# A two-layer recurrent-memory transformer on one core: half 0's last bank in one copy, half 1's scores together, the last 64 dimensions of the ordinary weighting as quarters of the array, up weights loaded sooner

## The chip, the cores and the metric

The kernel runs on one NeuronCore of a Trainium2 chip. The metric is the device time of one execution in microseconds (us), as the median of several runs. The engines are called as the profile calls them: PE is TensorE's matmuls, PEld its weight loads, DVE is VectorE, ACT is ScalarE, POOL is GpSimd and SP is SyncE, which issues most DMAs.

## The reference

There are two layers, each an attention with a recurrent memory and then a gated feed-forward block, over 2048 tokens of 448 numbers.

```
def _A_ref(x, mem0, Wq, Wk, Wv, Wo, seg_len):        # H=16 heads of 256, M=8 memory tokens, segments of 32
    for s in range(n_seg):                            # 64 segments, one after another
        h = concatenate([mem, x[segment s]])          # 40 tokens
        q, k, v = h @ Wq, h @ Wk, h @ Wv
        p = softmax(where(mask, q k^T * scale, -1e9)) # all may look at the 8 memory tokens, causal otherwise
        o = (p @ v) @ Wo
        mem = o[:, :8];  out_s = o[:, 8:]             # the memory goes to the next segment
def _B_ref(x, W_gate, W_up, W_down):                  # 448 -> 1792 -> 448
    g = x @ W_gate;  g = g * (g > 0);  return (g * (x @ W_up)) @ W_down
x = x + A(layernorm(x));  x = x + B(layernorm(x));  x = x + A(layernorm(x));  x = x + B(layernorm(x))
```

The memory makes the segments a chain: segment s+1 needs the output of segment s.

## The kernel before, in words

**Folding.** Before the first segment the weights of each head are multiplied together: Wq Wk^T for the scores (`A_sb`) and Wv Wo for the output (`B_sb`). That is the first stage, about 75 us: loop one over `p` (eight pairs of heads, transposes of Wq and Wk, products `aps`, `mxw`), loop two over `p` (transposes of Wv, products `bps`). `load_wo` fetches a piece of Wo (448 KB) on POOL's queue ahead of loop two, `flips` allocates the transposed tiles `qT`, `kT`, `vT` from a ring of buffers under the tag `tT`.

**Steps.** Then `step(g, ...)` runs for g = 0 to 68. Chain 0 is layer one at segment g, chain 1 is layer two at segment g - 4 (`LAG`), so the steps 4 to 63 carry two chains (80 token columns) and the eight steps 0 to 3 and 64 to 67 carry one (40 columns). Every second step from g = 3 on is a feed step: it carries `ff`, an object `Feed`, whose feed-forward work is placed by hand between the attention's. The other steps are called ordinary here.

**One step on PE**, in order of issue, which `in_order` fixes for PE and `InOrder` for DVE and ACT:
- `project(0, ...)`: the projections of the heads of half 0, five PSUM banks `prj` of up to six head tiles each, called by their first tile 0, 6, 24, 12, 18. Each bank is copied to `TQ` or `TZ` by ACT or DVE. In a feed step the bank 18 of half 0 (`quick`) is copied in two pieces by ACT, the first after three of its six tiles. In a feed step the layernorm's `residual` and `norm` for the feed-forward lie in this stretch (`otp`, then DVE, POOL and DVE again: `xn`).
- `project_early(1, ...)`: a 64-row part of half 1, as pairs of row tiles of the array.
- `late()`: `weigh_x(1)` of the step before, that is the ordinary weighting of half 1: `y1` (two passes of 256 columns for each chain) and `y2` (one of 256, then two of 128 columns for the last 64 dimensions, `hk[rows, 3]` and `hk[rows, 4]`, whose other halves are zero). Chain 0 uses array rows 0 to 63, chain 1 rows 64 to 127, so the two chains' matmuls run side by side.
- `project(1, ...)`, with the memory's scores of half 0 (`scores_m(0)`, bank `Sm`) and their softmax in between.
- `scores_x(0)` (bank `Sx`), the weighting by memory `weigh_m(0)` (`ya`, `yb`), `scores_m(1)`, `scores_x(1)`. Scores run over `KD = (0, 1, 3, 2)`; index 2 needs the last bank's copy.
- In a feed step the gate and up products (`open_rows`, `gate_up`, PSUM tiles `ups`, `gps`, result `hh`) and the down product (`dps`); in both kinds the output projection (`ox`, 84 matmuls for each half, and `o3` in 64-column tiles), with transposes `pps` of the softmax (`flipped`) in between.
- `finish()`, `project_early(0)` of the next step, and `weigh_x(0)`.

**Banks and loads.** `bank(...)` gives out the eight PSUM banks in the program's order, each matmul that opens a bank waits for the copy that last read it. The weights of the feed-forward come in 28 `pieces`, one for each call of `next_piece()`, on SP's queue: 7 of W_up, 7 of W_gate (224 KB each), 14 of W_down (112 KB each). `spread` makes each wait for the PE instruction before it in the program.

Of the kernel before, what the change touches and what calls it, by code (L numbers as in the profile page):

```python
# [8 lines left out]
BF = mybir.dt.bfloat16  # L9
# [8 lines left out]
NP = 8  # L18
# [41 lines left out]
def build_kernel(ctx, tc, A_x, A_mem0, A_Wq, A_Wk, A_Wv, A_Wo, B_W_gate, B_W_up, B_W_down, out,  # L60
# [150 lines left out]
    B_sb = glob.tile([P, 2, NT, DM], BF, name="B_sb")  # L211

    hTb = []
    for i in range(2):
# [58 lines left out]
    with tc.tile_pool(name="pre", bufs=6) as pre:  # L273
# [33 lines left out]
        def flips(src, p, name):  # L307
            nat = load_nat(src, p, nc.sync)
            o = pre.tile([P, 4, 512], BF, tag="tT", name=name)

            def half(e2):
                tp = bank([P, 2, 512], BF, "tpw")
                n = 3 if src is Wv else 4
                for kd in range(n):
                    for e in range(2):
                        tr(tp[:, e, kd * 128:(kd + 1) * 128],
                           nat[:, kd, (2 * e2 + e) * 128:(2 * e2 + e + 1) * 128], ident[:])
                n = DM if src is Wk else 128 * n
# [30 lines left out]
        def load_wo(p):  # L349
            wos.append(pre.tile([P, 4, DM], BF, tag="wo", name="wo", bufs=4))  # L350
            spread(nc.gpsimd.dma_start(wos[-1][:], Wo[:, 4 * p:4 * p + 4, :]))
# [6 lines left out]
        for p in range(NP):  # L358
# [28 lines left out]
            share(A_sb[0:64, 3, hf, 24 + p4, :], mx_ps[0:64, 3, :], 128, (1.28, 0.85))  # L387
            if p >= 4:
                load_wo(p - 4)
            if p == 1:  # L390
# [4 lines left out]
        for p in range(NP):  # L395
            hf, p4 = divmod(p, 4)
            vT = ready
            ready, todo = flips(Wv, p + 1, "vT") if p + 1 < NP else (None, [])
            wo = wos.pop(0)
            for eo in range(2):  # L400
                for kd in range(3):
                    bps = bank([P, 512], F32, "bps")
                    for t in range(2):
                        e = 2 * eo + t
                        mm(bps[:, 0:DM], vT[:, e, kd * 128:(kd + 1) * 128], wo[:, e, :],
                           start=(t == 0), stop=(t == 1))
                    share(B_sb[:, hf, tidx(kd, eo, p4), 0:DM], bps[:, 0:DM], DM, (1.28, 0.85))
                    if kd == 1 and todo:
                        todo.pop(0)()
            bps = bank([P, 512], F32, "bps")  # L410
            for t in range(2):
                for eo in range(2):
                    e = 2 * eo + t
                    mm(bps[64 * eo:64 * eo + 64, 0:DM], v3[:, p, e, :], wo[:, e, :],
                       start=(t == 0), stop=(t == 1), tile_position=(0, 64 * eo))
            share(B_sb[:, hf, 24 + p4, 0:DM], bps[:, 0:DM], DM, (1.28, 0.85))
            if p + 4 < NP:
                load_wo(p + 4)

# [23 lines left out]
    Wg_sb = main.tile([P, 4, F], BF, name="Wg_sb")  # L443
    Wu_sb = main.tile([P, 4, F], BF, name="Wu_sb")
    Wd_sb = main.tile([P, FT, DM], BF, name="Wd_sb")
    pieces = []
    for dst, src in ((Wu_sb, B_W_up), (Wg_sb, B_W_gate)):
        for k in range(3):
            for cols in (slice(0, F // 2), slice(F // 2, F)):
                pieces.append((dst[:, k, cols], src[128 * k:128 * k + 128, cols]))  # L450
        pieces.append((dst[FR[src is B_W_gate], 3, :], src[384:448]))
    for f in range(FT):
        pieces.append((Wd_sb[:, f, :], B_W_down[128 * f:128 * f + 128]))

    def next_piece():

        if pieces:
            spread(nc.sync.dma_start(*pieces.pop(0)))


# [133 lines left out]
    def project(hf, chains, hb, j, banks, pre={}, busy=False, first=None, inside=None):  # L594

        n = L * len(chains)
        for i0, k in banks:
            ps = pre[i0] if i0 in pre else bank([P, 512], F32, "prj")
            two = len(chains) == 2
            quick = busy and not hf and i0 == 18  # L600

            def copies(eng, rows, T, a, b):
                T = T.rearrange("p g (t q) -> p t g q", q=16)
                if two:
                    evac(eng, T, ps[rows, a * n:b * n].rearrange("p (t g q) -> p t g q", t=b - a, q=16))
                    return
                c = chains[0]
                src = ps[rows, a * n:b * n].rearrange("p (t w) -> p t w", t=b - a)
# [5 lines left out]
            def tq(a, b):  # L614
                return TQ[hf][:].rearrange("p g u w -> p g (u w)")[:, :, 16 * (i0 + a):16 * (i0 + b)]

            for i in range(k):
                if inside is not None and i == 4:
                    inside()
                if quick and i == 3:  # L620
                    copies(act, slice(0, P), tq(0, 3), 0, 3)
                for kd in range(3 if i0 in pre else 4):
# [7 lines left out]
            if i0 < 24:  # L630
                a = 3 if quick else 0
                copies(act if (i0 != 6 if busy and hf else i0 % 12) else dve, slice(0, P), tq(a, k), a, k)
            else:
                copies(act if busy else dve, slice(0, 64), TZ[hf][0:64, :, 0:64], 0, k)
                copies(act, slice(64, 128), TZ[hf][64:128, :, 64:128], 0, k)
            if i0 in (6, 18):
# [43 lines left out]
    def step(g, ff, pre, late):  # L680
# [28 lines left out]

        def scores_m(hf):  # L710
            if not ms:
                return (lambda: None,) * 3
            Sp = bank([P, 2, L], F32, "Sm", 1100)
            for kd in KD:
                mm(Sp[:, :, :], queries(hf, 2, kd), moving(hb, j, kd, (0, 1)), start=(kd == KD[0]), stop=(kd == KD[-1]))
            return softmax(Sp, 2, PM[hf], blk[:], f"m{hf}")

        def scores_x(hf):
            Sp = bank([P, 4, L], F32, "Sx", 2500 if hf == 0 else 3500 if ff is None else 8000)
            both = len(chains) == 2  # L720
            if not both:
                mm(Sp[:, :, :], ident[:], maskS[:], start=True, stop=False, skip_group_check=True)
            for half in range(2):
                for c in chains:
                    for kd in KD:
                        mm(Sp[:, 2 * half + c, :], queries(hf, 3 * c + half, kd), moving(hb, j, kd, (c,)),
                           start=(both and kd == KD[0]), stop=(kd == KD[-1]), skip_group_check=True)
            return softmax(Sp, 4, PX[hf], None, f"x{hf}", maskS[:] if len(chains) == 2 else None)

# [12 lines left out]

        def weigh_x(hf, hk, PT):

# [13 lines left out]
            for c in chains:  # L758
                keep(act if c == 0 or len(chains) == 1 else dve, c, 0, y1[c][:])
            y2 = {c: bank([P, 384], F32, f"y2_{c}", 1300) for c in chains}  # L760
            for c in chains:
                rows = slice(64 * c, 64 * c + L)
                mm(y2[c][:, 0:256], hk[rows, 2, :], PT[rows, 0:256], start=True, stop=True)
            for eo in range(2):
                for c in chains:
                    rows = slice(64 * c, 64 * c + L)
                    mm(y2[c][:, 256:384], hk[rows, 3 + eo, :],
                       PT[rows, :].rearrange("p (e o w) -> p e o w", e=2, o=2)[:, :, eo, :],
                       start=(eo == 0), stop=(eo == 1))
            for c in chains:  # L770
# [76 lines left out]
        pre1 = project_early(1, chains, hb, j)  # L847
        if late is not None:
            late()
        if len(chains) == 1:  # L850
            m0 = scores_m(0)
            m0[0]()
            m0[1]()
        project(1, chains, hb, j, BANKS[1][0:1], pre1, True)
        if len(chains) == 2:
            m0 = scores_m(0)
            m0[0]()
            m0[1]()
        project(1, chains, hb, j, BANKS[1][1:2], pre1, True, m0[2])
# [11 lines left out]
        if ff is not None:  # L871
            ff.xposed_out()
        x0 = scores_x(0)
        weigh_m(0, hk, pm)
        m1 = scores_m(1)
        m1[0]()
        m1[1]()
        x1 = scores_x(1)
        x0[0]()
# [44 lines left out]
        else:  # L924
# [24 lines left out]
        weigh_x(0, hk, px0)  # L949
        return pre, lambda: weigh_x(1, hk, px1)  # L950

# [91 lines left out]
```

## Time and profile before

| | |
|---|---|
| median of 3 runs | 1606.29 us (1604.5 to 1607.28) |
| profiled execution, its own time | 1606.33 us |
| span of its profile | 1604.4 us |
| PE busy, share of the span | 1573.1 us, 98% |
| PE weight loads | 1445.3 us, 90% |
| DVE, ACT, POOL busy | 1133.0, 757.4, 77.4 us |
| TensorE clock granted | full throughout |
| PE, longest class of waits | 16.6 us, 33 times, projections behind ACT's copy to TQ |

The profile's span is 1.93 us shorter than its execution's time. In a timeline row the columns are start (us from the span's start), length (us), engine, line, operation, tiles, array rows * columns used, shape, count, and in brackets the idle time before it and what ended it. A row of xN stands for N instructions in a row; matmuls overlap, a single one of 80 columns is shown as 0.20 us long, but the next starts far earlier. The idle time in brackets is counted from the shown end of the matmul before, so the start of a row says more than the bracket. All matmuls have one line, that of the helper `mm` (L143), transposes another (L151), and copies that of `InOrder` (L101), so rows are told apart by tiles.

### The profile page before, as it was taken

Reading aid. Unit: us, or ns where it says so; the run is one execution under the profiler, and the core shown is the slowest. Engines: PE = TensorE matmul, PEld = TensorE weight load, DVE = VectorE, ACT = ScalarE, POOL = GpSimd, SP = SyncE. Lnnn points to the kernel's source line nnn. Section 1 sums busy time; section 2 is a strip of 40 time slices with the busy share of each in tenths; the row PEclk is TensorE's granted clock in tenths of the full one; section 3 lists DMA queues with packets and bytes.
Section 4 is the critical chain, followed back from the end, with each engine's and each line's share of the span. In section 5 each row is a group of like instructions: output and inputs, shape, how many; then the busy total and the mean of one; then the engine's idle time right before and its main releaser. Section 6 shows DMA issues by size and latency. Waiting matters only on the chain.

```text
span 1604.4 us, 89783 instructions
## 1 busy us (share of the span) xinstructions
PE 1573.1 (98%) x41132; PEld 1445.3 (90%) x41132; DVE 1133.0 (71%) x3706; ACT 757.4 (47%) x2126; POOL 77.4 (5%) x172
## 2 busy tenths in 40 slices
PE   9999999999999999999999999999999999999998
PEld 6688999999999999999999999999999999999897
DVE  8766777777677777776777777767777777667765
ACT  5644444454444444544444445444444454444443
POOL 3200000000000000000000000000000000000000
PEclk9999999999999999999999999999999999999999
DMA  8530000000000000000000000000000000000000
GB/s 242 163 107 15 8 9 9 10 4 9 9 10 9 9 9 9 4 9 10 9 9 9 9 8 5 10 9 9 9 9 9 7 5 10 9 8 6 7 7 6
DMA packets 27755, 33.12 MB, mean 21 GB/s; under 512 B 3560, under 2 KB 26480, under 8 KB 27376
## 3 DMA queue, kind: packets, MB, share of 16 engines
q1 hardware_dynamic: 26288, 23.70, 5.3%
q8 instruction: 321, 5.26, 1.3%
q0 software_dynamic: 1088, 3.68, 0.8%
q14 instruction: 58, 0.48, 0.1%
HBM read 23.70 MB, written 1.84 MB: 16 GB/s over the span
## 4 chain that ended last, share of the span: by engine, by line
PE 96%; ACT 1%; DVE 1%; issue 1%; DMA 0%; SPq 0%; POOLq 0%; ACTq 0%; POOL 0%
PE prj L143 31%; PE ox L143 25%; PE ups L143 7%; PE dps L143 5%; PE gps L143 5%; PE o L143 5%; PE y L143 4%; PE Sx L143 3%; PE pps L151 2%; PE Sm L143 2%; PE bps L143 1%; PE aps L143 1%; PE tpw L151 1%; PE ya L143 1%; PE tps L151 1%; PE yb L143 1%
## 5 line engine op out<-in xcount | busy, mean ns | idle before, releaser
L143 PE MATMUL prj<-hT,A_sb 128*128 128x80 bf16 (+3 forms) x15232 | 547.1, 199 | 17.3 <-ACT TQ L101 16.6
L143 PEld LDWEIGHTS <-A_sb 128*128 128x128 bf16 (+1 forms) x15232 | 500.8, 99 | 42.9 <-issue 21.2
L143 PEld LDWEIGHTS <-B_sb 128*128 128x128 bf16 (+1 forms) x15232 | 490.6, 103 | 14.5 <-issue 1.0
L143 PE MATMUL ox<-Y,B_sb 128*128 128x80 bf16 (+3 forms) x11424 | 440.3, 199 | 0.9 <-issue 0.9
L101 ACT CAST TQ<-prj 128x480 bf16<-128x480 f32 (+5 forms) x416 | 189.6, 466 | 111.4 <-PE prj L143 101.4
L101 DVE CAST Y<-y 128x256 bf16<-128x256 f32 x376 | 151.4, 457 | 55.5 <-PE y L143 55.4
L101 ACT CAST Y<-y 128x512 bf16<-128x512 f32 (+2 forms) x392 | 136.6, 419 | 103.4 <-PE y L143 103.2
L101 ACT ACTIVATE se<-se 128x80 f32<-128x80 f32 (+1 forms) x270 | 81.9, 303 | 165.5 <-DVE se L101 161.2
L143 PE MATMUL gps<-xT,Wg_sb 128*128 128x128 bf16 (+3 forms) x1904 | 133.9, 216 | 0.0
L101 DVE CAST TQ<-prj 128x480 bf16<-128x480 f32 (+1 forms) x228 | 128.4, 572 | 7.5 <-PE prj L143 7.0
L143 PE MATMUL ups<-xT,Wu_sb 128*128 128x128 bf16 (+3 forms) x1904 | 132.3, 216 | 0.5 <-DVE xT L101 0.5
L101 DVE SCALAR_TENSOR_TENSOR hh<-gps,ut 128x512 bf16<-128x512 f32 (+2 forms) x136 | 80.2, 592 | 47.6 <-PE ya L143 41.4
L143 PEld LDWEIGHTS <-Wu_sb 128*128 128x128 bf16 (+1 forms) x1904 | 105.0, 97 | 8.0
L143 PEld LDWEIGHTS <-hk 40*128 40x128 bf16 (+1 forms) x1950 | 99.4, 96 | 10.7 <-issue 2.5
L143 PEld LDWEIGHTS <-Wg_sb 128*128 128x128 bf16 (+1 forms) x1904 | 106.9, 97 | 0.5 <-issue 0.5
L101 ACT CAST TZ<-prj 64x320 bf16<-64x320 f32 (+2 forms) x264 | 96.8, 377 | 17.2 <-DVE TZ L101 13.6
L101 ACT COPY os<-o 64x16 f32<-64x16 f32 (+3 forms) x135 | 25.8, 191 | 162.2 <-PE o L143 160.6
L101 DVE TENSOR_REDUCE ssum<-se 128x2 f32<-128x80 f32 (+1 forms) x270 | 73.7, 273 | 37.5 <-ACT se L101 37.5
L143 PE MATMUL dps<-Wd_sb,hh 128*128 128x448 bf16 (+1 forms) x476 | 93.1, 353 | 0.0
L143 PEld LDWEIGHTS <-TQ 128*128 128x128 bf16 x1938 | 87.1, 97 | 6.0 <-issue 0.4
L143 PE MATMUL y<-PT,hk 40*128 40x256 bf16 (+1 forms) x1280 | 86.7, 248 | 1.6 <-ACT PT L101 1.0
L235 POOL TENSOR_SCALAR rstd<-mv 128x1 f32<-128x1 f32 x67 | 14.8, 221 | 1467.2 <-DVE mv L101 1467.2
(118 smaller groups left out, 1920.0 us busy)
## 6 DMA issues: line engine op xcount, KB each, us to landing
wo<-in_A_Wo_dram POOLq DMA_DIRECT2D x8, 448.0 KB, 4.6
nat<-in_A_Wq_dram SPq DMA_DIRECT2D x8, 384.0 KB, 4.9
nat<-in_A_Wk_dram SPq DMA_DIRECT2D x8, 384.0 KB, 5.0
nat<-in_A_Wv_dram SPq DMA_DIRECT2D x8, 384.0 KB, 5.7
xa<-in_A_x_dram SPq DMA_DIRECT2D x32, 56.0 KB, 2.2
xa<-xp SPq DMA_DIRECT2D x32, 56.0 KB, 1.9
out_dram<-xa SPq DMA_DIRECT2D x32, 56.0 KB, 2.3
xp<-in_A_x_dram SPq DMA_DIRECT2D x30, 56.0 KB, 2.6
```

Of the source, the lines that this page charges most:

```text
L101: r = f(*a, **k)
L143: in_order(nc.tensor.matmul(out, lhsT, rhs, **k))
L151: in_order(nc.tensor.transpose(out, src, idn))
L235: nc.gpsimd.tensor_scalar(out=rstd[:], in0=mv[:, 1:2], scalar1=EPS, scalar2=None, op0=ALU.add)
```

## The change

Five edits, all of the order or the shape of work; what is computed stays.

- `project`: `quick` is gone; bank 18 of half 0 is copied whole in feed steps too, after its sixth tile.
- `scores` takes the place of `scores_m` and `scores_x`. For half 1 it issues memory and ordinary scores together: indices 0, 1, 3 of `Sm`, then of all groups of `Sx`, then index 2 of `Sm`, then of `Sx`.
- `weigh_x`: the last 64 dimensions use 64x64 quarters of the array: stationary `hk[rows, 3, 0:64]`, the even and the odd heads in column halves 0 and 64, so four matmuls of 128 columns stand in four quarters.
- In one-chain steps the memory's scores of half 0 (`memory_0`) stand inside `weigh_x(1)`, between `y1` and `y2`, and `late_flip` is 23 in place of 22.
- `Wu_sb` moves to the pool of the whole kernel, its seven pieces are issued in loop two of the folding (two for each `p` from 3 on), and the pieces of W_gate and W_down take the earlier calls. For the room, `tT` has 4 buffers in place of 6, `wo` has 3 in place of 4, and Wo's pieces are asked for one pair of heads later. In the built program SP's queue still has all loads of Wv ahead of the first piece of W_up.

```diff
+    Wu_sb = glob.tile([P, 4, F], BF, name="Wu_sb")
...
+    pieces = weights(Wu_sb, B_W_up)
...
-            o = pre.tile([P, 4, 512], BF, tag="tT", name=name)
+            o = pre.tile([P, 4, 512], BF, tag="tT", name=name, bufs=4)
...
-            wos.append(pre.tile([P, 4, DM], BF, tag="wo", name="wo", bufs=4))
+            wos.append(pre.tile([P, 4, DM], BF, tag="wo", name="wo", bufs=3))
...
-            if p >= 4:
-                load_wo(p - 4)
+            if p >= 5:
+                load_wo(p - 5)
...
-            if p + 4 < NP:
-                load_wo(p + 4)
+            if p + 3 < NP:
+                load_wo(p + 3)
+            if p >= 3:
+                next_piece()
+                next_piece()
...
+    pieces += weights(Wg_sb, B_W_gate)
...
-            quick = busy and not hf and i0 == 18
...
-                if quick and i == 3:
-                    copies(act, slice(0, P), tq(0, 3), 0, 3)
...
+            if m and x:
+                mem(KD[:3])
+                mask()
+                own(KD[:3])
+                mem(KD[3:])
+                own(KD[3:])
...
             for eo in range(2):
                 for c in chains:
                     rows = slice(64 * c, 64 * c + L)
-                    mm(y2[c][:, 256:384], hk[rows, 3 + eo, :],
+                    mm(y2[c][64 * eo:64 * eo + 64, 256:384], hk[rows, 3, 0:64],
                        PT[rows, :].rearrange("p (e o w) -> p e o w", e=2, o=2)[:, :, eo, :],
-                       start=(eo == 0), stop=(eo == 1))
+                       start=True, stop=True, tile_position=(64 * c, 64 * eo), skip_group_check=True)
...
         if late is not None:
-            late()
-        if len(chains) == 1:
-            m0 = scores_m(0)
-            m0[0]()
-            m0[1]()
+            late(memory_0 if len(chains) == 1 else None)
+        if len(chains) == 1 and late is None:
+            memory_0()
...
-        x0 = scores_x(0)
+        _, x0 = scores(0, False, True)
         weigh_m(0, hk, pm)
-        m1 = scores_m(1)
+        m1, x1 = scores(1, True, True)
         m1[0]()
         m1[1]()
-        x1 = scores_x(1)
...
-            late_flip = 23 if hi - lo == W else 22
+            late_flip = 23
```

More of the change, by code (lines that the diff above doesn't have):

```diff
@@ L211, in build_kernel, with weights, next_piece @@
     B_sb = glob.tile([P, 2, NT, DM], BF, name="B_sb")
+    Wu_sb = glob.tile([P, 4, F], BF, name="Wu_sb")
+    def weights(dst, src):
+        return [(dst[:, k, cols], src[128 * k:128 * k + 128, cols])
+                for k in range(3) for cols in (slice(0, F // 2), slice(F // 2, F))] + [
+                    (dst[FR[src is B_W_gate], 3, :], src[384:448])]
+    pieces = weights(Wu_sb, B_W_up)
+    def next_piece():
+        if pieces:
+            spread(nc.sync.dma_start(*pieces.pop(0)))
     hTb = []
@@ L443, in build_kernel @@
     Wg_sb = main.tile([P, 4, F], BF, name="Wg_sb")
-    Wu_sb = main.tile([P, 4, F], BF, name="Wu_sb")
+    pieces += weights(Wg_sb, B_W_gate)
     Wd_sb = main.tile([P, FT, DM], BF, name="Wd_sb")
[L446 to L451, printed above, removed]
     for f in range(FT):
         pieces.append((Wd_sb[:, f, :], B_W_down[128 * f:128 * f + 128]))
-    def next_piece():
-        if pieces:
-            spread(nc.sync.dma_start(*pieces.pop(0)))
     class Feed:
@@ L599, in project, with copies @@
             two = len(chains) == 2
-            quick = busy and not hf and i0 == 18
-            def copies(eng, rows, T, a, b):
+            def copies(eng, rows, T):
                 T = T.rearrange("p g (t q) -> p t g q", q=16)
                 if two:
-                    evac(eng, T, ps[rows, a * n:b * n].rearrange("p (t g q) -> p t g q", t=b - a, q=16))
+                    evac(eng, T, ps[rows, 0:k * n].rearrange("p (t g q) -> p t g q", t=k, q=16))
                     return
                 c = chains[0]
-                src = ps[rows, a * n:b * n].rearrange("p (t w) -> p t w", t=b - a)
+                src = ps[rows, 0:k * n].rearrange("p (t w) -> p t w", t=k)
                 x, m = (0, SEG) if c == 0 else (MEM, 0)
@@ L612, in copies @@
                      src[:, :, x:x + SEG].rearrange("p t (g q) -> p t g q", q=16))
-            def tq(a, b):
-                return TQ[hf][:].rearrange("p g u w -> p g (u w)")[:, :, 16 * (i0 + a):16 * (i0 + b)]
             for i in range(k):
@@ L630, in project @@
             if i0 < 24:
-                a = 3 if quick else 0
-                copies(act if (i0 != 6 if busy and hf else i0 % 12) else dve, slice(0, P), tq(a, k), a, k)
-            else:
-                copies(act if busy else dve, slice(0, 64), TZ[hf][0:64, :, 0:64], 0, k)
-                copies(act, slice(64, 128), TZ[hf][64:128, :, 64:128], 0, k)
+                T = TQ[hf][:].rearrange("p g u w -> p g (u w)")[:, :, 16 * i0:16 * (i0 + k)]
+                copies(act if (i0 != 6 if busy and hf else i0 % 12) else dve, slice(0, P), T)
+            else:
+                copies(act if busy else dve, slice(0, 64), TZ[hf][0:64, :, 0:64])
+                copies(act, slice(64, 128), TZ[hf][64:128, :, 64:128])
             if i0 in (6, 18):
@@ L708, in hk_make, with scores, mem, own @@
             return hk
-        def scores_m(hf):
+        def scores(hf, m, x):
             if not ms:
[L712 to L719, printed above, removed]
-            both = len(chains) == 2
[L721 to L728, printed above, removed]
+                m = False
+            both = len(chains) == 2
+            Sm = bank([P, 2, L], F32, "Sm", 1100) if m else None
+            Sx = bank([P, 4, L], F32, "Sx", 2500 if hf == 0 else 3500 if ff is None else 8000) if x else None
+            groups = [(half, c) for half in range(2) for c in chains]
+            def mem(kds):
+                for kd in kds:
+                    mm(Sm[:, :, :], queries(hf, 2, kd), moving(hb, j, kd, (0, 1)),
+                       start=(kd == KD[0]), stop=(kd == KD[-1]), skip_group_check=True)
+            def own(kds):
+                for half, c in groups:
+                    for kd in kds:
+                        mm(Sx[:, 2 * half + c, :], queries(hf, 3 * c + half, kd), moving(hb, j, kd, (c,)),
+                           start=(both and kd == KD[0] and (half, c) == groups[0]), stop=(kd == KD[-1]),
+                           skip_group_check=True)
+            def mask():
+                if not both:
+                    mm(Sx[:, :, :], ident[:], maskS[:], start=True, stop=False, skip_group_check=True)
+            if m and x:
[4 more added lines that the diff above has]
+                own(KD[3:])
+            elif m:
+                mem(KD)
+            elif x:
+                mask()
+                own(KD)
+            sm = softmax(Sm, 2, PM[hf], blk[:], f"m{hf}") if m else (lambda: None,) * 3
+            sx = softmax(Sx, 4, PX[hf], None, f"x{hf}", maskS[:] if both else None) if x else None
+            return sm, sx
@@ L741, in weigh_m, with weigh_x @@
             act.copy(YB[hf][:, 16:28, M0:M0 + 16], yb[:].rearrange("p (t q) -> p t q", q=16))
-        def weigh_x(hf, hk, PT):
+        def weigh_x(hf, hk, PT, between=None):
             def keep(eng, c, t0, src):
@@ L759, in weigh_x @@
                 keep(act if c == 0 or len(chains) == 1 else dve, c, 0, y1[c][:])
+            if between is not None:
+                between()
             y2 = {c: bank([P, 384], F32, f"y2_{c}", 1300) for c in chains}
@@ L847, in step, with memory_0 @@
         pre1 = project_early(1, chains, hb, j)
-        if late is not None:
-            late()
-        if len(chains) == 1:
-            m0 = scores_m(0)
+        m0 = None
+        def memory_0():
+            nonlocal m0
+            m0, _ = scores(0, True, False)
             m0[0]()
             m0[1]()
+        if late is not None:
+            late(memory_0 if len(chains) == 1 else None)
+        if len(chains) == 1 and late is None:
+            memory_0()
         project(1, chains, hb, j, BANKS[1][0:1], pre1, True)
         if len(chains) == 2:
-            m0 = scores_m(0)
-            m0[0]()
-            m0[1]()
+            memory_0()
         project(1, chains, hb, j, BANKS[1][1:2], pre1, True, m0[2])
@@ L949, in step @@
         weigh_x(0, hk, px0)
-        return pre, lambda: weigh_x(1, hk, px1)
+        return pre, lambda between: weigh_x(1, hk, px1, between)
     nsteps = nseg + LAG
```

## The prediction

> **What bounds the kernel now.** First the page, for the span, the busy times and the chain of work that ended last.
>
> ```profile
> span 1604.4 us, 89783 instructions
> PE 1573.1 (98%) x41132; PEld 1445.3 (90%) x41132; DVE 1133.0 (71%) x3706; ACT 757.4 (47%) x2126; POOL 77.4 (5%) x172
> PE 96%; ACT 1%; DVE 1%; issue 1%; DMA 0%; SPq 0%; POOLq 0%; ACTq 0%; POOL 0%
> ```
>
> PE is the end. Time is won only where PE waits or where it has fewer passes. So next the waits, for PE alone:
>
> ```profile
> PE prj L143 <- ACT TQ L101: 16.6, 33, 0.5
> ```
>
> This is the only class that comes back in every feed step (33 of them); no other class on PE is over 1.2 us. Then the timeline of one feed step around it:
>
> ```profile
> 710.81 1.21 PE L143 MATMUL prj<-hT,A_sb 128*128 128x80 bf16 x29
> 712.11 0.36 ACT L101 CAST TQ<-prj 128x240 bf16<-128x240 f32 x1
> 712.52 1.02 PE L143 MATMUL prj<-hT,A_sb 128*128 128x80 bf16 x33 [0.50 <-ACT TQ L101]
> 712.78 0.61 DVE L101 TENSOR_SCALAR xn<-xa,mv,rstd 128x448 bf16<-128x448 bf16 x2 [0.39 <-POOL rstd L236]
> 713.04 0.36 ACT L101 CAST TQ<-prj 128x240 bf16<-128x240 f32 x1 [0.57 <-PE prj L143]
> 713.37 0.61 PE L143 MATMUL y<-PT,hk 40*128 40x256 bf16 x10
> 713.82 1.22 DVE L101 CAST Y<-y 128x512 bf16<-128x512 f32 x3 [0.44 <-PE y L143]
> 713.91 0.82 PE L143 MATMUL prj<-hT,A_sb 128*128 128x80 bf16 x18
> ```
>
> PE stops after three of the six tiles of bank 18 until ACT has read them (712.47), since its next matmul writes the same bank. And the same place in an ordinary step, where the bank is already copied whole:
>
> ```profile
> 739.40 1.13 PE L143 MATMUL prj<-hT,A_sb 128*128 128x80 bf16 x36
> 740.03 0.56 ACT L101 CAST TQ<-prj 128x480 bf16<-128x480 f32 x1 [0.35 <-PE prj L143]
> 740.37 0.65 PE L143 MATMUL y<-PT,hk 40*128 40x256 bf16 x10
> 740.95 0.42 PE L143 MATMUL prj<-hT,A_sb 128*128 128x80 bf16 x7
> ```
>
> **1. `quick` goes.** A matmul of 80 columns is shown 0.20 us long, but x29 take 1.21, so they start (1.21-0.20)/28 = 0.036 us apart. The last before the stop starts at 710.81+1.01 = 711.82, the next at 712.52: 0.70, of which 0.04 is work. The bracket's 0.50 counts from the shown end; PE loses 0.67. Over 33 feed steps: -22.1 us.
>
> What is late next? Two things in the same step. (a) The second bank of `y2` is the bank just copied. The whole copy starts 0.23 after the last matmul of the bank, as in the ordinary step, and takes 0.56 against 0.36. The ordinary step shows the price: from the first `y` to the next `prj` 740.95-740.37 = 0.58, in the feed step 713.91-713.37 = 0.54. So +0.04 to +0.05. (b) DVE is in `xn` until 713.39, set by the layernorm's chain through POOL, which does not move. Its copy of `y1`, now ready for at 713.82-0.67 = 713.15, starts 0.25 late and ends at 714.09. The first matmul into that bank (bank 24 of half 1) starts in the trace at 714.70, after the change at 714.70-0.67+0.05+0.04 (edit 2) = 714.12, and a wait needs some 0.05 from the end of the copy. So +0.02. Together +0.07 on 33 steps, +2.3.
>
> **2. Quarters.** Each call of `weigh_x` loses one pass of 128 columns, 0.055 us (the four `tps` transposes of 128 columns start 0.056 apart), and gains one change of the array's tile shape, from 64x128 to 64x64, ahead of the change back to 128x128 that it has already. The trace has no 64x64 tile, so I take the price from the nearest changes:
>
> ```profile
> 707.12 0.49 PE L143 MATMUL ox<-Y,B_sb 128*128 128x80 bf16 x9
> 707.54 0.60 PE L143 MATMUL prj<-hT,A_sb 64*128 64x80 bf16 x24
> 703.06 1.19 PE L143 MATMUL o<-Y,B_sb 128*64 128x80 bf16 x56
> 704.18 0.60 PE L143 MATMUL ox<-Y,B_sb 128*128 128x80 bf16 x12
> ```
>
> Nine matmuls 0.036 apart from 707.12 would end their turn at 707.44; the row tiles start at 707.54: 0.10. The `o` pairs are again 0.036 apart, the last pair starts at 703.06+1.19-0.20 = 704.05, and `ox` follows at 704.18 and not 704.09: 0.09 to 0.10 for column tiles. The step from 128*64 back to 64*128 tiles (`bps` to `prj`, 75.69) also pays. So rows and columns cost alike, and I take 0.095: net +0.04 per call. There are 2x60 calls with two chains and 16 with one, 136: +5.4 us. Ends: no price for this change -0.055, that is -7.5; a price plus two passes in turn because four quarters do not all run side by side +0.10, that is +13.6. The weight loads speak for side by side: the two column tiles of `o` load in turns and still start as pairs 3 ns apart.
>
> The Trainium skill, "TensorEngine Tiling (Array Packing)", section Key Properties, speaks against this edit: changing the tiling mode, not just the tile, drains the engine. By that rule the quarters lose, and the 0.10 at each change in the rows above agrees; by the same page's "Theoretical Speedup" table alone the edit would be a gain, which is the -7.5 end.
>
> **3. Scores of half 1 together.** The last index of `Sm` waits for bank 18's copy:
>
> ```profile
> 718.19 0.20 PE L143 MATMUL Sm<-hT,TZ 128*128 128x80 bf16 x1
> 718.36 0.21 PE L143 MATMUL Sm<-hT,TQ 128*128 128x80 bf16 x1
> ```
>
> 0.17 against 0.036, so 0.14 in a feed step; in the ordinary step 745.01 to 745.13, so 0.08. After the change twelve matmuls of 0.025, 0.30 us, stand in between and cover it. But `Sm` is then finished some 0.2 later, and DVE's softmax with it. In a feed step DVE runs without a gap from there to `hh` (721.61 to 722.29), and the `gps` that reuses its bank starts at 722.53: DVE comes 0.33 later against PE, the slack is 0.24 less 0.05, so 0.13 of the 0.14 is given back. In the ordinary step `PM1` is ready at 747.66, its transpose at 748.05; it eats the slack and costs 0.01 to 0.02. So -0.01 on 30 feed steps and -0.06 on 30 ordinary ones: -2.1 us.
>
> **4. One-chain steps.** The memory's scores between `y1` and `y2` take away a wait of `Sm` on ACT's copy of `Y` (once, 0.4 by the waits); the later `Sm` of half 1 and the later flip shift a transpose that waits on `PM1` by under 0.1 in five steps. Taken as 0, within 0.5 either way.
>
> **5. Loads.** In the one-chain steps PE's own instruction queue runs dry at times while weights stream in:
>
> ```profile
> 89.94 0.34 PE L143 MATMUL ox<-Y,B_sb 128*128 128x40 bf16 x7 [0.86 <-issue]
> 105.77 0.27 PE L151 MATMUL pps<-ident,PX 128*128 128x128 bf16 x2 [0.56 <-issue]
> ```
>
> There are five such gaps between 85 and 106 us; start to start they lose 3.4 us. They stand beside pieces of W_up and W_gate (224 KB); the step from 106 to 121 us, with pieces of W_down (112 KB) alone, has none. After the change W_gate takes W_up's calls and W_down those of W_gate, so half as much flows from 86 on. I take -1.5, from 0 to -3.4. The cover of the moved pieces is loop two of the folding, where DMA is at 0.24 of its share and PE is in `bps` passes of 0.189 us. SP's queue puts them behind all loads of Wv, so nothing on it waits for them but the next pieces. On POOL's queue Wo is asked for two passes of loop two ahead (2x3.55 us) and lands in 4.0 to 4.3 there; the first, asked for at 39.9, landed at 47.3 and is needed at 48. If it came late it would cost up to 1 us. POOL's clearing of `hk`, `Y1` and `hh` moves from 63.3 to some 67 and takes 5.1, needed from 77 on: 0. The smaller `tT` ring still holds this pass's and the next pass's two tiles: 0.
>
> **Sum.** -22.1+2.3+5.4-2.1+0-1.5 = -18.0. The profiled execution took 1606.33, span 1604.4 and 1.9 around it, and the median is 1606.29, so no correction: 1588.3 us, 1.1% faster. What a measurement can tell from no change is about 0.2%, 3.2 us.
>
> **Rivals.**
> - *The quarters switch for free.* For: both shapes have 64 rows, only the columns change. Against: the 128x64 column tiles pay too. Then 136x0.095 = 12.9 less: 1575.4. Chance 0.10.
> - *The wait moves.* DVE (71% busy) becomes the bound in the feed step: `y1`'s copy behind `xn`, then the softmax. If every later wait kept DVE's lag of 0.42 of the 0.67, 33x0.42 = 13.9 comes back: 1602. Against: the slack of 0.41 at the transpose of `PM0` (717.19, ready 716.77). Chance 0.10.
> - *Slower: four quarter loads in a row.* A tile shape's first weight load can't be hidden behind the shape before it; if the four loads (`LDWEIGHTS` of 128x64 from `B_sb`: 113 ns mean) followed one another, each call would pay 0.095 and three more of 0.10 before its one pass: +0.34, 136 times +46, and 1588.3+46-5.4 = 1629. It decides from (18.0+5.4)/136 = 0.17 per call on. Against: the `o` pairs. Chance 0.05. The same section of the Trainium skill says under Restrictions that column tiling disables fast weight load; no run here shows a 64x64 load.
>
> **Numbers.** Forecast 0.73, rivals 0.10, 0.10, 0.05, unknown 0.02. The forecast's own range is 1582 to 1595 by the ends of edits 2, 4 and 5. With the free switch nearly and half of the moved wait it is 1577 to 1598. Faster 0.92, same 0.03, slower 0.05.
>
> **What would show it.** The class PE prj behind ACT TQ is gone from PE's waits; a feed step is 0.53 shorter, an ordinary one within 0.05 of before. From the first `y` to the next `prj` both kinds take 0.58 to 0.63; 0.49 would be the free switch, 0.9 the loads in a row. No wait over 0.05 ahead of the last `Sm`; a new one of about 0.13 at the second `gps`. Fewer gaps by issue between 85 and 106. Wrong, if PE waits anew for DVE's `Y` or `PM`, or for Wo around 48 us.

## The result

The changed kernel takes 1595.29 us (median of 4 runs, 1593.72 to 1596.08). The kernel before, run beside it, takes 1606.47. The ratio is 0.9931, with an interval from 0.9914 to 0.9948: 11 us faster, where 18 were forecast. The profiled execution took 1594.63 us, its span is 1592.6, so the two profiles differ by 11.8 us.

The page after, its busy times and the chain that ended last:

```profile
span 1592.6 us, 89753 instructions
...
PE 1578.0 (99%) x41132; PEld 1435.4 (90%) x41132; DVE 1133.2 (71%) x3706; ACT 753.6 (47%) x2090; POOL 77.4 (5%) x172
...
PE 97%; DVE 1%; issue 0%; ACT 0%; SPq 0%; DMA 0%; POOLq 0%; POOL 0%; ACTq 0%
```

PE is still the end. Its busy time rose by 4.9 us while the span fell, a first sign that something made its work longer. ACT has 36 instructions fewer: the second pieces of bank 18's copy. The waits of PE, the longest classes:

```profile
PE junk L143 <- DVE still L170: 1.2, 1, 1.2
PE y L143 <- ACT PT L101: 1.0, 2, 0.5
PE pps L151 <- DVE PM L101: 1.0, 2, 0.5
```

The class of 16.6 us, projections behind ACT's `TQ`, is gone, and nothing of its size has come. What came instead is small and hides in starts, not in this view. The timeline of the feed step that the prediction showed:

```profile
705.89 2.56 PE L143 MATMUL prj<-hT,A_sb 128*128 128x80 bf16 x76
...
707.31 0.66 DVE L101 CAST TQ<-prj 128x480 bf16<-128x480 f32 x1
...
708.01 0.56 ACT L101 CAST TQ<-prj 128x480 bf16<-128x480 f32 x1 [0.45 <-PE prj L143]
...
708.29 0.78 PE L143 MATMUL y<-PT,hk 40*128 40x256 bf16 x10
...
708.81 0.11 PEld L143 LDWEIGHTS <-hk 40*64 40x64 bf16 x4 [0.31 <-issue]
...
709.00 0.82 PE L143 MATMUL prj<-hT,A_sb 128*128 128x80 bf16 x18
```

PE now runs through bank 18 without a stop. From the first `y` to the next `prj` it takes 709.00-708.29 = 0.71, where 0.54 was measured before and 0.58 to 0.63 forecast. ACT's whole copy ends at 708.57, and the second bank of `y2` has to wait for it. The same stretch in the other call, `weigh_x(0)` at the end of the same step, where the second bank waits some 0.03 in both kernels:

```profile
730.93 0.72 PE L143 MATMUL y<-PT,hk 40*128 40x256 bf16 x10
731.58 1.47 PE L143 MATMUL prj<-hT,A_sb 128*128 128x80 bf16 x36
```

0.65 us against 0.59 before. The new wait at the second `gps`, in DVE's timeline and in PE's:

```profile
716.86 1.28 DVE L101 SCALAR_TENSOR_TENSOR hh<-gps,ut 128x512 bf16<-128x512 f32 x2
```
```profile
717.42 0.22 PE L143 MATMUL ups<-xT,Wu_sb 64*128 64x128 bf16 x1
717.42 0.22 PE L143 MATMUL gps<-xT,Wg_sb 64*128 64x128 bf16 x1
717.47 0.22 PE L143 MATMUL ups<-xT,Wu_sb 64*128 64x128 bf16 x1
717.60 0.21 PE L143 MATMUL gps<-xT,Wg_sb 64*128 64x128 bf16 x1
```

`ups` and `gps` are row tiles that run side by side, here at 717.42 both. The pair after it is torn apart, 717.47 and 717.60: `gps` waits for the first of the two `hh` (716.86 plus half of 1.28). The bracket shows nothing, since the matmul before is drawn longer than the gap; only the starts do.

Measured from the first `kps` of a step (the transposes near its start) to that of the next, with two chains, a feed step fell from 27.88 to 27.42 us on most steps (-0.445 in the mean) and an ordinary step rose from 18.03 to 18.09 (+0.064).

### The profile page after: what moved, and what is told of

Its sections match the earlier page's. It is cut to its first block, busy times and chain, and to the rows that moved or that the text cites. A ratio compares the mean times of both kernels' runs of the same rounds, so it can differ in the third digit from the quotient of the medians.

```text
span 1592.6 us, 89753 instructions
## 1 busy us (share of the span) xinstructions
PE 1578.0 (99%) x41132; PEld 1435.4 (90%) x41132; DVE 1133.2 (71%) x3706; ACT 753.6 (47%) x2090; POOL 77.4 (5%) x172
## 4 chain that ended last, share of the span: by engine, by line
PE 97%; DVE 1%; issue 0%; ACT 0%; SPq 0%; DMA 0%; POOLq 0%; POOL 0%; ACTq 0%
PE prj L143 31%; PE ox L143 25%; PE ups L143 7%; PE dps L143 5%; PE gps L143 5%; PE y L143 5%; PE o L143 5%; PE Sx L143 3%; PE pps L151 2%; PE bps L143 1%; PE aps L143 1%; PE Sm L143 1%; PE tpw L151 1%; PE ya L143 1%; PE yb L143 1%; PE kps L151 1%
## 5 line engine op out<-in xcount | busy, mean ns | idle before, releaser
L143 PE MATMUL prj<-hT,A_sb 128*128 128x80 bf16 (+3 forms) x15232 | 541.6, 199 | 0.5 <-issue 0.5
L101 ACT CAST TQ<-prj 128x480 bf16<-128x480 f32 (+1 forms) x380 | 184.2, 497 | 113.3 <-PE prj L143 103.0
L143 PE MATMUL gps<-xT,Wg_sb 128*128 128x128 bf16 (+3 forms) x1904 | 137.2, 215 | 0.0
L143 PEld LDWEIGHTS <-hk 40*128 40x128 bf16 (+2 forms) x1950 | 92.5, 98 | 35.8 <-issue 22.8
L143 PE MATMUL y<-PT,hk 40*128 40x256 bf16 (+1 forms) x1280 | 100.4, 258 | 1.9 <-ACT PT L101 1.0
L101 ACT COPY PT<-pps 128x256 bf16<-128x256 bf16 (+1 forms) x136 | 47.2, 347 | 81.8 <-PE pps L151 77.6
```

The costliest lines, as they stand in the source:

```text
L101: r = f(*a, **k)
L143: in_order(nc.tensor.matmul(out, lhsT, rhs, **k))
```

## The experiments

**Each edit alone in the kernel before.** Four runs take the parts of the forecast one by one.

```diff
-            quick = busy and not hf and i0 == 18
+            quick = False
```

> The kernel before, with only bank 18 of half 0 copied whole in feed steps. Theory A (read from the trace after: the shortfall against the forecast is mostly the quarters, and each feed step keeps 0.67 less 0.10 that the second bank of y2 now waits for the copy): 33 x -0.56 = -18.6 us, ratio 0.9884; from the first y to the next prj 0.64 in a feed step against 0.54 before. Theory B (the shortfall lies here, DVE's lag gives much of the 0.67 back later in the step): -12 to -14 us, ratio 0.992, with new waits of PE on DVE (Y, PM or hh) in feed steps. As predicted: -19.8.

Measured: 1590.70 us against 1608.28, ratio 0.9889 (0.9875 to 0.9902), 17.8 us faster. Theory A holds. A feed step is 0.555 shorter, an ordinary one 0.003. So `quick` was worth nearly all of its 0.67 and DVE is no new bound. What is given back is 0.10, not 0.07, in one place, `y2`'s second bank. The timeline of the kernel with this edit alone:

```profile
705.09 0.56 ACT L101 CAST TQ<-prj 128x480 bf16<-128x480 f32 x1 [0.45 <-PE prj L143]
...
705.37 0.71 PE L143 MATMUL y<-PT,hk 40*128 40x256 bf16 x10
...
706.01 0.82 PE L143 MATMUL prj<-hT,A_sb 128*128 128x80 bf16 x18
```

0.64 from `y` to `prj`, where it was 0.54. The copy runs from 705.09 to 705.65; within the x10 row, `y2`'s second bank starts at 705.70, 0.107 behind its partner instead of 0.003. In the ordinary step of before the copy starts 0.34 ahead of the first `y`, here 0.28.

```diff
-                    mm(y2[c][:, 256:384], hk[rows, 3 + eo, :],
+                    mm(y2[c][64 * eo:64 * eo + 64, 256:384], hk[rows, 3, 0:64],
...
-                       start=(eo == 0), stop=(eo == 1))
+                       start=True, stop=True, tile_position=(64 * c, 64 * eo), skip_group_check=True)
```

> The kernel before, with only the last 64 dimensions of the ordinary weighting as 64x64 quarters. Theory A: 136 calls at +0.066 (one more change of tile shape 0.09, the change back from 64x64 some 0.02 dearer, one pass of 0.055 less) = +9.0 us, ratio 1.0056. Theory B: the quarters are nearly neutral, the added time being covered by waits that were there anyway: 0 to +2 us, ratio 1.000 to 1.001. As predicted: +5.4 us, ratio 1.0034. Without a price for the change of shape: -7.5 us, 0.9953.

Measured: 1618.12 us, ratio 1.0058 (1.0045 to 1.0070), 9.3 us slower. Theory A holds. Both kinds of step are 0.134 longer, 0.067 for each call. The call at the end of an ordinary step:

```profile
712.97 0.72 PE L143 MATMUL y<-PT,hk 40*128 40x256 bf16 x10
713.62 1.47 PE L143 MATMUL prj<-hT,A_sb 128*128 128x80 bf16 x36
```

It is 0.65 from `y` to `prj`, as in the changed kernel. A step has two such calls, so 0.134; in the changed kernel the scores give part of it back in an ordinary step, and +0.064 is left.

```diff
-        x0 = scores_x(0)
+        _, x0 = scores(0, False, True)
...
-        m1 = scores_m(1)
+        m1, x1 = scores(1, True, True)
```

> The kernel before, with only half 1's two kinds of scores issued together. Theory A: feed step -0.14 at the last Sm and +0.12 back at the second gps, ordinary step -0.08 and +0.02 back at the first ox: 30 x -0.02 and 30 x -0.066, -2.6 us, ratio 0.9984. Theory B: the later softmax of half 1 also costs at later transposes: 0. If the cover were free in both kinds of step: -6.6 us.

Measured: 1604.93 us, ratio 0.9983 (0.9974 to 0.9992), 2.7 us faster. Theory A holds: feed -0.035, ordinary -0.078. The wait ahead of the last `Sm` (0.14) is gone, and `gps` waits 0.11 for `hh`, where 0.12 was expected.

```diff
+    pieces = weights(Wu_sb, B_W_up)
...
+            if p >= 3:
+                next_piece()
+                next_piece()
...
+    pieces += weights(Wg_sb, B_W_gate)
...
-    pieces = []
```

(in short: the loads, pools and ring sizes of the change, and nothing else of it)

> The kernel before, with only the up weights loaded in the folding, and the smaller rings. Prediction: gaps by issue on PE between 77 and 122 us fall from 3.4 to about 1.9, -1.5 us, ratio 0.9991. Rival: the gaps come from how the instruction queue refills in one-chain steps, whatever is loaded: they move and do not shrink, 0 us.

Measured: 1607.14 us, ratio 0.9992 (0.9983 to 1.0001). The time alone cannot be told from no change. The gaps by issue between 76 and 123 us say more. In the changed kernel:

```profile
PE ox L143 <- issue: 0.9, 1, 0.9
PE prj L143 <- issue: 0.5, 1, 0.5
```

and with the loads alone:

```profile
PE prj L143 <- issue: 0.3, 1, 0.3
PE Sx L143 <- issue: 0.2, 1, 0.2
```

Five profiles with the loads as before add up to 2.3 to 3.7 us of such gaps in this window (mean 2.7), eight with the early loads to 0.3 to 1.9 (mean 1.1). So the early loads are worth 1.6 us, less sharply than forecast: one gap of 0.9 stands at 89.95 as it did before, with half as much weight in flight.

Where the gaps stand says what they are. Between 76 and 123 us the thirteen profiles have 50 of them of more than 0.15 us. Counted in PE's instructions (matmuls and weight loads together) all 50 lie at whole multiples of 256 from one another, to within two, and each ends 1.2 to 1.8 us after the end of a packet of the DMA queue q8. The page of before has this line for that queue:

```profile
q8 instruction: 321, 5.26, 1.3%
```

These are 321 packets of 16 KB, one for every 256 of PE's 82264 instructions. So PE lacked its own next instructions there, as the forecast had it. That the pieces of weights are what holds these packets up is argued from the totals alone.

**The change without its quarters.** The two lines of the second experiment put back in the changed kernel.

> The changed kernel with the last 64 dimensions back in 64x128 row tiles; all else of the change kept. Theory A (each call pays 0.066 for the quarters): 9.0 us less than the changed kernel, ratio to before 0.9875. Theory B (the shortfall is DVE's lag, which the quarters' time only covers, so PE would wait for it instead): within 3 us of the changed kernel, ratio 0.991 to 0.993.

Measured: 1587.00 us against 1607.68, ratio 0.9870 (0.9857 to 0.9884). Theory A holds. This beats both kernels; its interval lies below that of the change. Feed steps -0.579, ordinary -0.073 against before: close to the sum of the first and third experiments (-0.590 and -0.081).

**What the quarters cost: the changes of shape.** The quarters are issued ahead of `y2`'s pass of 256 columns, so that the array goes through 64x128, 64x64, 64x128 and 128x128 tiles.

```diff
-            for c in chains:
-                rows = slice(64 * c, 64 * c + L)
-                mm(y2[c][:, 0:256], hk[rows, 2, :], PT[rows, 0:256], start=True, stop=True)
             for eo in range(2):
...
+            for c in chains:
+                rows = slice(64 * c, 64 * c + L)
+                mm(y2[c][:, 0:256], hk[rows, 2, :], PT[rows, 0:256], start=True, stop=True, skip_group_check=True)
```

> The changed kernel with the quarters ahead of y2's pass of 256 columns, so that the array goes 64x128, 64x64, 64x128, 128x128: one more change of shape, the same matmuls. Theory A (every change between shapes costs about 0.09 to 0.12, both ways): from the first quarter to the pass of 256 columns 0.16 to 0.18 us in place of 0.06; in the late calls this lies beside the 0.10 that y2's second bank waits, in the calls at the step's end it does not, so +3 us to +6 us on the changed kernel, ratio to before 0.995 to 0.997. Rival (the 0.09 is the quarters' own first loads, and the way back between two shapes of 64 rows is free): 0.06 between them, no loss, up to -3 us, ratio 0.991 to 0.993.

Measured: 1602.33 us, ratio 0.9964 (0.9951 to 0.9976). Theory A holds: one more change, 0.077 more in a feed step and 0.121 in an ordinary one than in the changed kernel. These are two calls each, and with two chains a part of the change falls into the wait for `y2`'s second bank; a call with one chain, which has no such wait, takes 0.104 more (0.694 in place of 0.590). `y1`'s last pass to the first quarter takes 0.196, of which 0.105 is the pass: 0.09 for the change between two shapes that both have 64 rows. From the last quarter to the next pass it takes 0.173; if the quarter counts as 0.055, that leaves 0.12.

**What the quarters cost: the passes.** All four quarters are issued twice (the first round's line is that of the added loop, L788).

> The changed kernel with the four quarter matmuls issued twice. Theory A (the four run side by side, the price is in the changes of shape): one more pass of 0.055 to 0.06 for each of 136 calls, +7.5 to +8 us, ratio to before 0.998. Rival (the quarters follow one another, or two by two): +0.11 to +0.22 per call, +15 to +30 us, ratio 1.002 to 1.012.

Measured: 1603.24 us, ratio 0.9974 (0.9964 to 0.9984); 0.11 more for each step than the changed kernel, 0.055 for each call, one pass and not four. The timeline of a call at a step's end (half 0):

```profile
707.03 0.11 PEld L788 LDWEIGHTS <-hk 40*64 40x64 bf16 x4
707.03 0.25 PE L788 MATMUL y<-PT,hk 40*64 40x128 bf16 x4
707.06 0.12 PEld L143 LDWEIGHTS <-hk 40*64 40x64 bf16 x4
707.11 0.23 PE L143 MATMUL y<-PT,hk 40*64 40x128 bf16 x4
707.27 1.46 PE L143 MATMUL prj<-hT,A_sb 128*128 128x80 bf16 x36
```

Four matmuls of 128 columns take one turn, and the second four's loads lie beside the first four's matmuls. The rival of loads in a row falls here. But the second round starts 0.08 after the first (707.03 to 707.11), not 0.055, and from the last quarter to `prj` it now takes 0.148, where the changed kernel takes 0.173.

**An attempt to hide the wait of `y2`'s bank.** In the version without quarters, `project_early` goes between `y1` and `y2` (in the call of `late()`, and in the weighting at the step's end).

```diff
-            late(memory_0 if len(chains) == 1 else None)
+            late(memory_0 if len(chains) == 1 else early_1)
...
+            weigh_x(0, hk, px0, early_0)
```

> A version that should beat both: the changed kernel without the quarters, and in two-chain steps project_early, which is in 64-row tiles too, stands between y1 and y2 of weigh_x, so that y2's second bank is free when PE comes to it. The waits in the late calls (0.10 in feed steps, 0.05 in ordinary ones) and the 0.03 of the calls at the step's end should go: 30 x 0.15 + 60 x 0.03 = 6 us less than the version without quarters, ratio to before 0.984. Rival: the wait moves on to the next bank or to DVE: no gain on the version without quarters, 0.9875.

Measured: 1607.97 us, ratio 1.0003 (0.9994 to 1.0011), 21 us slower than the version without quarters, where 6 us faster were expected. In the call of `late()`, `y2` comes no later than before, since `y1` and the early projections only change places. At the step's end the banks are given out anew, and `y2`'s second bank is that of `y1`. The timeline there:

```profile
735.81 0.59 PE L143 MATMUL prj<-hT,A_sb 64*128 64x80 bf16 x24
736.01 0.59 ACT L101 CAST Y<-y 128x512 bf16<-128x512 f32 x1 [1.34 <-PE y L143]
...
736.24 0.78 PE L143 MATMUL y<-PT,hk 40*128 40x256 bf16 x6
```

Six matmuls that need 0.4 take 0.78: all but the first wait for ACT's copy of `y1`, until 736.60. The wait is 0.40 to 0.46 each time, 60 times, 26 us.

**The wait for `hh`.** In the version without quarters, the ordinary weighting's softmax steps stand ahead of `Sm`'s in feed steps, so that DVE has work while the later `Sm` comes.

```diff
+        if swap:
+            x0[0]()
+            x0[1]()
         m1[0]()
         m1[1]()
-        x0[0]()
+        if not swap:
+            x0[0]()
...
-            x0[1]()
+            x0[2]()
             m1[2]()
-            x0[2]()
```

> The change without its quarters, and in the feed steps the ordinary weighting's maximum, negation and exponentials stand on DVE and ACT ahead of those of the other chain's product Sm, instead of DVE waiting for Sm first. Theory A (the wait of 0.116 us that TensorE takes up at the second chain's scores of a feed step, for the weighting hh, comes from the place of hh behind the late Sm): 30 x 0.116 = 3.5 us off the version without quarters, about 0.985 of the kernel before. Theory B (Sm's own chain, now behind, holds TensorE up just as long at its weighted sum): no gain, 0.987. Slower than 0.988 would mean that Sm's exponentials were needed sooner.

Measured: 1585.07 us, ratio 0.9856 (0.9843 to 0.9870). In the timeline of the version without quarters the pair is torn apart as in the changed kernel:

```profile
714.03 0.22 PE L143 MATMUL ups<-xT,Wu_sb 64*128 64x128 bf16 x1
714.15 0.21 PE L143 MATMUL gps<-xT,Wg_sb 64*128 64x128 bf16 x1
```

and with the new order it is closed to 0.01:

```profile
714.17 0.22 PE L143 MATMUL ups<-xT,Wu_sb 64*128 64x128 bf16 x1
714.18 0.21 PE L143 MATMUL gps<-xT,Wg_sb 64*128 64x128 bf16 x1
```

Nearly every two-chain feed step from g = 7 on is 0.10 shorter than without the edit, so theory A holds there, about 3 us. But the sum is 2 us at most, since `PM` comes late in the first steps. The class in PE's waits, with the new order:

```profile
PE pps L151 <- DVE PM L101: 2.5, 3, 1.1
```

**The one-chain edit alone**, in the kernel before.

```diff
-            late()
-        if len(chains) == 1:
-            m0 = scores_m(0)
+            late(memory_0 if len(chains) == 1 else None)
...
-            late_flip = 23 if hi - lo == W else 22
+            late_flip = 23
```

> The kernel before with the one-chain edit alone: the next weighted sum's scores between the two halves of y2, and its late copies moved by one. Theory A (the half of TensorE's idle that it fills is given back at the next product, as the prediction had it): 0 us within 0.5, ratio 0.9995 to 1.0005. Theory B (the later Sm makes the one-chain steps wait longer, 0.1 us at some five steps and more): 0.5 to 1 us slower, ratio 1.0003 to 1.0007. Neither can be told from the other by the time alone; the gaps ahead of the second weighting's scores and products in the first 75 us of the trace decide.

Measured: 1609.11 us, ratio 1.0005 (0.9996 to 1.0014); the span is 1.0 us longer. The time can't tell it from nothing, the rows can. One call of `weigh_x(1)` in the kernel before goes from its first `y` to `prj` in 95.31-94.63 = 0.68. The same call in the timeline of this run:

```profile
93.39 0.38 PE L143 MATMUL y<-PT,hk 40*128 40x256 bf16 x2
93.70 0.25 PE L143 MATMUL Sm<-hT,TQ 128*128 128x80 bf16 x2
93.78 0.20 PE L143 MATMUL Sm<-hT,TZ 128*128 128x80 bf16 x1
93.82 0.20 PE L143 MATMUL Sm<-hT,TQ 128*128 128x80 bf16 x1
93.95 0.39 PE L143 MATMUL y<-PT,hk 40*128 40x256 bf16 x3
94.28 0.89 PE L143 MATMUL prj<-hT,A_sb 128*128 128x40 bf16 x29
```

It takes 0.89. The `Sm` of 128x128 between two stretches of 64x128 makes three changes of shape out of one: two more of 0.09 to 0.10, six times. This is neither theory's mechanism, though it comes to about theory B's size: in five of the six calls the steps keep the 0.2, in step 64 the transpose after the call starts only 0.03 later.

**The parts that won, together**: no quarters, `memory_0` back behind `y2`, the softmax order of the experiment before the last from g = 9 on.

> Built from the runs before: no quarters, the memory's scores of half 0 back behind y2 in one-chain steps, and the ordinary weighting's softmax ahead in the feed steps from g = 9 on only, where all steps carry two chains. Theory A (each one-chain call of the edit pays two more changes of the array's tile shape, 0.19 us, in six or seven calls; and the early softmax loses 0.9 and 0.7 us in steps 3 and 5, where PE waits for PM): about 1.0 + 1.4 us less than the version with the early softmax everywhere, ratio about 0.984. Theory B (the longer one-chain steps come from where PE's instruction queue runs dry, which moves from run to run): no gain but for the 1.4 us, and steps 64 to 67 as long as in the one-chain edit alone, that is 0.8 us longer than in the kernel before.

Measured: 1583.75 us against 1608.09, ratio 0.9844 (0.9830 to 0.9857): the fastest version, 24 us below the kernel before. It lies clear of the changed kernel; from the version without quarters and the one with the softmax order everywhere the time alone does not part it. Against the latter, steps 3 and 5 together are 0.6 shorter, where 1.4 was expected. Steps 64 to 66 together are 0.58 shorter, which looks like theory A's 3x0.19 and is not: in steps 64 and 65 the transpose after the call starts at the same time to 0.03, so only the call of step 66 keeps its 0.21, and 0.34 more is a gap by issue that falls into the step after. So theory A's price is in the rows of every call, but without `quick` not every step pays it.

## Why the prediction was right or wrong

The direction, the bound and the mechanisms of the parts that win held. The time lies in the wide range of 1577 to 1598 and 0.3 us above the forecast's own range of 1582 to 1595; that one is narrower than its source, since the ends given for the quarters alone reach from 1575.4 to 1596.5. The forecast of 1588.3 is 7 us too low. The parts, each measured alone, against the terms of the sum (us, with the interval from the ratio):

| term | forecast | measured alone |
|---|---|---|
| 1 `quick` | -19.8 | -17.8 (-20.1 to -15.8) |
| 2 quarters | +5.4 | +9.3 (+7.2 to +11.3) |
| 3 scores | -2.1 | -2.7 (-4.2 to -1.3) |
| 4 one-chain | 0 | +0.8 (-0.6 to +2.3) |
| 5 loads | -1.5 | -1.3 (-2.7 to +0.2) |
| sum | -18.0 | -11.7; the change itself -11.1 (-13.8 to -8.4) |

The parts add up to the whole, so nothing interacts that the time could show. The fourth and the fifth can't be told from nothing by the time; for them the rows speak.

1. **`quick`** was right to a tenth. The 0.67 came back in full: 0.555 for the step, and 0.104 lost at the bank. Of the +0.07, the DVE part (+0.02, `y1`'s copy behind `xn`) did not show: in the changed kernel that copy ends at 709.55 and its reader starts at 709.79. The bank's part was 0.10 and not 0.045, since the price was read from the ordinary step, where ACT starts its copy 0.24 after the start of the bank's last matmul; in the feed step it starts 0.29 after it. In the built program that copy has its wait for PE as an instruction of its own on ACT, 0.056 ahead of it in the trace, and then a second wait, which the ordinary step's has not; that this is the 0.055 was not tried alone.

2. **The quarters** are the mis-sized term: "net +0.04 per call" measured 0.067, which is 3.9 us of the 7. Going in costs 0.09, as taken, and one pass less saves 0.055, as taken. The step that failed is "gains one change [...], ahead of the change back to 128x128 that it has already": it leaves the rest of the call as it was. In the run of the quarters alone, in the call of `late()` in a feed step, where nothing else waits, the first quarter starts 0.093 later than the pass in its place did, one pass of 0.056 is gone, and from the start of the last round to `prj` it takes 0.182 in place of 0.152: 0.093-0.056+0.030 = 0.067. It is not shown that the way back as such is dearer. With the quarters doubled the way from the last quarter to `prj` is 0.148, as it was from the last 64x128 pair before, and the surplus of 0.025 lies between the two rounds. So a round of quarters that follows a change costs more than its pass of 0.055; why stays open. The number of loads is not the reason, since a call with one chain, of two quarters a round, has the same 0.08 between its rounds. The free-switch rival fell with the same run, and the rival of loads in a row with the doubled quarters. The Trainium skill, "TensorEngine Tiling (Array Packing)", section Key Properties, says that a change of the tiling mode drains the engine. The runs here agree: each change costs time, also where both modes have 64 rows (0.09 us), and the one-chain run shows it where the prediction did not apply it (0.89 against 0.68 us for a call).

3. **The scores** were right: 0.14 won, 0.10 to 0.11 given back at `gps` (0.13 forecast), 0.078 won in the ordinary step (0.06 forecast).

4. **The one-chain steps**: the step "Taken as 0" failed. It weighed waits alone and did not count changes of the tile shape, though the same text priced one at 0.095. Two more are 0.2 in each of six calls, 1.2 us; step 64 takes its own up, which leaves 1.0.

5. **The loads**: right in size and in mechanism, as far as the gaps show it. "Half as much flows from 86 on" was not enough to remove the gap at 89.95, though; that gap, too, stands where PE's next 256 instructions were due.

Of what was to show it: the class of waits went, no wait stands ahead of the last `Sm`, the wait at the second `gps` is 0.12, the gaps by issue fell from five to two, and nothing waits for Wo. Of its signs of being wrong one came, small: PE's wait for `PM` rose from 0.3 to 1.0 us, in steps 4 and 5 alone. Outside its bounds were the stretch from `y` to `prj` (0.71 and 0.65 where 0.58 to 0.63 was given), the feed step (-0.445 where -0.53 was given) and the ordinary step (+0.064 where 0.05 was given), through term 2 and the bank.

## What to carry to other kernels

Count every change of the tile shape as a price, 0.09 to 0.12 us here, in every edit that moves or splits matmuls, not only in the one that is about shapes; a tiled stretch that saves one pass of 0.055 loses. An edit that is a bundle is worth taking apart: the quarters cost 9 us and the one-chain edit alone about 1 us by its rows, and without these two and with the new softmax order the kernel gains 1.6% instead of 0.7%. And where an engine is nearly always busy, read starts: the waits that decided here, 0.10 to 0.12 each, are in no bracket and in no class of waits.

## What was not expected of the hardware

- A round of 64x64 quarters that comes first after a change of shape costs more than its pass: 0.08 and not 0.055 to a second round, and 0.172 to `prj` or 0.173 to a 64x128 pass where a second round, or a 64x128 pair, takes 0.148.
- PE's gaps by issue in the one-chain steps move from run to run even with the same loads (2.3 to 3.7 us in all in five profiles), so one profile's gaps are no price for an edit that touches them. But the places are fixed: all 50 lie at multiples of 256 of PE's instructions from one another.
- In five of the thirteen profiles, those of the loads alone, the quarters alone, the quarters first, the quarters twice and the last version, the record of the clock has 3.4 us at half clock some 22 us before the end, and PE's last step is 1.5 to 2.0 us longer. The loads alone are an example: their profile's span is 1604.7 us, no shorter than before, though 2.1 us of gaps are gone. So a difference under 2 us between two profiles is read here from the steps ahead of that place, not from the spans.
